# Decode attention with a gated FFN on one core: w_down as 13 rows in each partition and its last 128 rows in 32 partitions; wo's second half in 128-column matmuls

## The chip, the cores and the metric

The kernel runs on one core of one Trainium2 chip. The metric is the device time of one execution in microseconds (us); lower is better. A core has a matrix engine (TensorE, PE), a vector engine (VectorE, DVE), a scalar engine (ScalarE, ACT), GpSimd (POOL), and SyncE (SP), which here issues every DMA. Sixteen DMA engines move data between the device memory (HBM) and the 128 partitions of SBUF; matmul results go to PSUM.

## What is computed

Four tokens (B = 4), width D = 512. A gate g mixes attention over a long cache with a GEGLU FFN:

```python
g = sigmoid((x * gate_w).sum(-1, keepdims=True))
q = (x @ wq).reshape(4, 1, 32, 128).transpose(0, 2, 1, 3)
p = softmax(einsum("bhqd,bhkd->bhqk", q, k_cache) * 128 ** -0.5)   # k_cache, v_cache: 4 x 32 x 4096 x 128
a = einsum("bhqk,bhkd->bhqd", p, v_cache).transpose(0, 2, 1, 3).reshape(4, 1, 4096) @ wo   # wo: 4096 x 512
b = (gelu(x @ w_gate) * (x @ w_up)) @ w_down                       # w_gate, w_up: 512 x 1792; w_down: 1792 x 512
return g * a + (1 - g) * b
```

Everything is float32. The two caches are 268 MB each and are read once; all weights together are about 28 MB.

## The kernel before

**Attention.** There are NT = 32 steps, one for each batch row and group of four heads. A step loads a K tile and a V tile of 8 MB (128 partitions of 64 KB: 32 partitions to a head, 128 rows of 128 to a partition). DVE multiplies K by the spread query (`products`, L213) and sums over the head dimension (`sums`, L219), in two parts: 32 rows that share their place with the next K tile first (`shared`), then 96. `max_a` and `soft_max` (L224 to L242) find the maximum through PE and let ACT make the exponentials. `pv` (L267) lets PE multiply them with V into PSUM. The query comes from wq at the start (L164, `q_spread`).

**One buffer.** Weights, K and V tiles lie at hand-placed columns of one SBUF tile, `big`. K(i) is at 0 or 12288, V at VA = 28672, each 16384 columns wide. w_gate and w_up stand in V's place until V(0) is loaded. At the end wo's first half is at W0 and w_down at D0 in V's place, wo's second half at W1 = 16384, and from ES = 24576 on come the spread attention outputs (`spread`, L318) and the copy of `wide` (`fold`); both of the last lie where K(31) was.

**Queues.** The order is written by hand; the framework adds semaphore waits where data or places depend on each other. SP issues the DMAs in program order: wq, x, K(0), gate_w, w_gate, w_up, K(1), then V and K in turn, and at the end `load_w(0)` (wo's first half, 4 MB), `load_d` (w_down, 3.5 MB) and `load_w(1)` (wo's second half). The last is cut into pieces of 8, 5, 2 and 1 of its 16 rows per partition (`WO_END`), each a DMA of its own.

**FFN.** In step 0, `ffn_up` (L330) multiplies x with w_gate and then w_up: the 1792 columns are cut into four blocks of FG = 448, one in each 32-partition column group of PSUM. ACT copies the result to `fu`; `ffn_gelu` (L338) makes the product on DVE; 14 DVE transposes (L349) turn it into `hT`, so that hidden unit 14 p + i lies in partition p of slice i. After that V(0) may be loaded over w_gate and w_up.

**The end.** PE's order after the last `pv` is: 16 matmuls of wo's first half, `turn(1)`, 14 of w_down (`ffn_down`, L351), 8 of wo's second half, all by `project_wide` (L251): 512 columns at once, the n-th into column group n % 4 of the PSUM tile `wide`, so that four groups hold partial sums. Then comes `project` (L257), which cuts the 512 columns into four of 128, one for each column group of `acc`: row 8 of wo's second half, `fold` (ACT copies `wide`, and a matmul with `stack` adds its four partial sums into `acc`), rows 9 to 15. DVE copies `acc`, SP stores it. A float32 matmul appears as two records and two weight loads in the trace.

Of the kernel before, what the change touches and what calls it, by code (L numbers as in the profile page):

```python
# [9 lines left out]
F32 = mybir.dt.float32  # L10
# [7 lines left out]
def tile_gated_mix(ctx: ExitStack, tc: tile.TileContext, x, kc, vc, wq, wo, w_gate, w_up, w_down, gate_w, out):  # L18
    nc = tc.nc
    P = 128  # L20
    B, H, S, D = kc.shape
    DM = x.shape[2]
    F = w_gate.shape[1]
    KC = DM // P
# [8 lines left out]
    RJ = 4  # L33
    BP = 2
    FG = F // 4
    FC = F // P
    HW = 16
    E = HW * D // P
    GW = HW // HT
    WO_END = (0, 8, 13, 15, E)  # L40
    scale = 1.0 / math.sqrt(D)
    c_gelu = math.sqrt(2.0 / math.pi)

# [6 lines left out]
    xT = head.tile([P, KC, 4, B, 8], F32)  # L50
    kv = ctx.enter_context(tc.tile_pool(name="kv", bufs=1))
    consts = ctx.enter_context(tc.tile_pool(name="consts", bufs=1))
# [9 lines left out]
    big = kv.tile([P, VA + TW], F32)  # L62
    Q0, F0, F1, W0, D0 = VA, VA, VA + KC * F, VA, VA + TW // 2
    W1, ES = TW, TW + TW // 2

    def place(a, n):
        return big[:, a:a + n]
# [16 lines left out]
    def load_f(s):  # L84
        nc.sync.dma_start(place((F0, F1)[s], KC * F), (w_gate, w_up)[s].rearrange("(p c) n -> p (c n)", c=KC))

    def load_d():
        nc.sync.dma_start(place(D0, FC * DM), w_down.rearrange("(p i) n -> p (i n)", i=FC))

    def load_w(w):  # L90
        t = place((W0, W1)[w], E * DM)
        src = wo[w * HW * D:(w + 1) * HW * D].rearrange("(p e) n -> p (e n)", e=E)
        ends = WO_END if w else (0, E)
        for e0, e1 in zip(ends, ends[1:]):
# [34 lines left out]
    xT = xT.rearrange("p c j b k -> p c (j b k)")  # L129
# [29 lines left out]
    for c in range(KC):  # L159
        w = place(Q0 + c * H * D, H * D)  # L160
# [11 lines left out]
    stack = consts.tile([P, 32], F32)  # L172
# [71 lines left out]

    acc = ps1.tile([P, C4], F32, name="acc")
    wide = ps1.tile([P, DM], F32, name="wide")
    NW = FC + E + WO_END[1]
    nw = iter(range(NW))


    def project_wide(t, w):  # L251
        n = next(nw)
        c = n % 4
        nc.tensor.matmul(wide[32 * c:32 * c + 32, :], t, w, start=n < 4, stop=n >= NW - 4)


    def project(t, w, start, stop):  # L257
        for c in range(4):
            nc.tensor.matmul(acc[32 * c:32 * c + 32, :], t, w[:, c * C4:(c + 1) * C4], start=start, stop=stop)  # L259


    def fold():
        t = place(ES + 2 * E * 32, DM)
        nc.scalar.activation(t, wide, AF.Copy)
        project(stack, t, False, False)

    def pv(i):  # L267
        b = i % BP
# [54 lines left out]
    def attended(w, e):  # L323
        return OTS[w][:, e * 32:e * 32 + 32], place((W0, W1)[w] + e * DM, DM)


    hT = consts.tile([P, FC, 32], F32)
    fu = place(VA + 2 * KC * F, 2 * DM).rearrange("p (s n) -> p s n", s=2)

    def ffn_up(s):  # L330
        ps = ps1.tile([P, FG], F32, name="q")
        for c in range(KC):
            for j in range(4):
                nc.tensor.matmul(ps[32 * j:32 * j + 32, :], xT[:, c, :32],  # L334
                                 place((F0, F1)[s] + c * F + j * FG, FG), start=c == 0, stop=c == KC - 1)
        nc.scalar.activation(fu[:, s, :FG], ps, AF.Copy)

    def ffn_gelu():  # L338
        x1 = fu[:, 0, :FG]
        t1, t2, t3, th, y, v = (place(F1 + a * DM, FG) for a in range(6))  # L340
        nc.vector.tensor_tensor(t1, x1, x1, op=OP.mult)
        nc.vector.tensor_scalar(t2, t1, 0.044715, 1.0, op0=OP.mult, op1=OP.add)
        nc.vector.tensor_tensor(t3, t2, x1, op=OP.mult)  # L343
        nc.scalar.activation(th, t3, AF.Tanh, scale=c_gelu)
        nc.vector.scalar_tensor_tensor(y, th, 1.0, x1, op0=OP.add, op1=OP.mult)  # L345
        nc.vector.scalar_tensor_tensor(v, y, half, fu[:, 1, :FG], op0=OP.mult, op1=OP.mult)  # L346

        for i in range(FC):
            nc.vector.transpose(hT[:, i, :], v[:, i::FC])  # L349

    def ffn_down():  # L351
        for f in range(FC):
            project_wide(hT[:, f, :], place(D0 + f * DM, DM))


    load_f(0)
# [2 lines left out]
    for i in range(NT):  # L359
# [12 lines left out]
        if i == 0:  # L372
            half, gmask = gates()
            ffn_up(0)
            ffn_up(1)
            ffn_gelu()
            load_v(0)
# [14 lines left out]
        if b == 1 and g + 1 < NG:  # L392
            q_spread(g + 1)
    load_w(0)
    load_d()
    load_w(1)
    spread(0)
# [8 lines left out]
    turned(1)  # L406
    spread(1)
    ffn_down()
    for e in range(WO_END[1]):
        project_wide(*attended(1, e))  # L410
    project(*attended(1, WO_END[1]), True, False)
    fold()
    for e in range(WO_END[1] + 1, E):
        project(*attended(1, e), False, e == E - 1)
    res = work.tile([P, C4], F32, name="res", bufs=1)
    nc.vector.tensor_copy(res, acc)  # L416
# [23 lines left out]
```

## Time and profile before

The median of three runs is 1313.91 us (1313.85 to 1314.07). The profiled execution took 1313.79 us; its span, from the first to the last instruction, is 1312.0 us.

| what | value | how to read it |
|---|---|---|
| run, span | 1313.79, 1312.0 us | 1.79 us lie outside the span |
| bytes moved | 565.07 MB in 10,711 packets | a packet is one contiguous run, 64 KB for K and V |
| mean rate | 431 GB/s | over the span |
| K and V loads | 32 + 32, 29.6 and 29.2 us from issue to landing | issued about 20 us apart, so that one waits behind the other |
| wo, first half | issued 1266.72, 23.2 us to landing | |
| w_down | issued 1270.12, 28.4 us to landing | |
| wo, second half | four DMAs from 1276.44 on; 27.0, 29.6 and 30.5 us for those of 2048, 1280 and 256 KB | the fourth is issued at 1277.8 |
| DVE | 1143.2 us | L213 and L219 are 555.8 and 555.4 of it |
| granted PE clock | 0.632 in the mean | 0.5 or 1.0 at any one time |

### The profile page before, as it was taken

The numbers are of one execution on the slowest core, as the hardware profiler recorded it, in microseconds if no ns is written. First come the engines' busy times: TensorE is split into PE (matmuls) and PEld (weight loads), VectorE is DVE, ScalarE is ACT, GpSimd is POOL, SyncE is SP. The second block draws the span as 40 slices with busy tenths as digits, with TensorE's granted clock in tenths as the row PEclk, the third lists the DMA queues.
The fourth block names the chain that finished last, engine by engine and source line by source line (L and its number), as shares of the span: only waits on it lengthen the run. The fifth ranks groups of instructions, "written<-read, shape, count | busy, mean of one in ns | idle before, by whom it ended". The sixth has DMA issues, their size and how long they took to land.

```text
span 1312.0 us, 6267 instructions
## 1 busy us (share of the span) xinstructions
PE 394.9 (30%) x2680; PEld 130.9 (10%) x2680; DVE 1143.2 (87%) x261; ACT 92.6 (7%) x321; POOL 0.7 (0%) x6
## 2 busy tenths in 40 slices
PE   2403323212333321333322232322123322122337
PEld 0101001000010000110001000100001000010012
DVE  1899889988899988988989988998889898898890
ACT  0000000000000100000000000000000000000010
POOL 0000000000000000000000000000000000000000
PEclk9656666556666555666655666665566666566668
DMA  9999999999999999999999999999999999999997
GB/s 416 428 436 442 422 440 424 440 442 428 438 428 434 438 426 444 434 430 432 434 438 432 438 428 436 428 438 434 434 442 422 444 426 436 440 428 440 426 429 338
DMA packets 10711, 565.07 MB, mean 431 GB/s; under 512 B 1320, under 2 KB 1336, under 8 KB 1596
## 3 DMA queue, kind: packets, MB, share of 16 engines
q1 hardware_dynamic: 10684, 564.68, 99.5%
q8 instruction: 21, 0.34, 0.1%
q14 instruction: 6, 0.05, 0.0%
HBM read 564.67 MB, written 0.01 MB: 430 GB/s over the span
## 4 chain that ended last, share of the span: by engine, by line
DMA 72%; DVE 26%; PE 1%; issue 0%; ACT 0%; SPq 0%; DVEq 0%
DMA big<-in_A_k_cache 66%; DVE sc L219 13%; DVE big L213 12%; DMA big<-in_A_wo 2%; DMA big<-in_B_w_up 2%; DMA big<-in_A_x 2%; PE po L164 1%; PE q L334 0%; PE acc L259 0%; DVE m L233 0%; DVE hT L349 0%; DVE m L226 0%; DVE big L346 0%; DVE big L345 0%; DVE big L343 0%
## 5 line engine op out<-in xcount | busy, mean ns | idle before, releaser
L213 DVE TENSOR_TENSOR big<-big,qb 128x4096 f32<-128x4096 f32 x64 | 555.8, 8684 | 103.1 <-DMA big<-in_A_k_cache 103.1
L219 DVE TENSOR_REDUCE sc<-big 128x32 f32<-128x4096 f32 x64 | 555.4, 8678 | 1.1
L272 PE MATMUL po<-big,PM 128*32 128x512 f32 x2048 | 295.9, 742 | 437.9 <-DMA big<-in_A_v_cache 435.4
L272 PEld LDWEIGHTS po<-big,PM 128*32 128x32 f32 x2048 | 80.8, 133 | 626.7 <-issue 624.2
L235 PE MATMUL sm<-m,ones 1*128 1x4 f32 x64 | 18.7, 360 | 218.4 <-DVE m L233 218.4
L228 PE MATMUL sm<-ident,m 128*1 128x128 f32 x32 | 11.9, 371 | 214.4 <-DVE m L226 180.3
L240 ACT ACTIVATE PM<-sc,nb 32x128 f32<-32x128 f32 x128 | 67.4, 526 | 2.6
L237 ACT ACTIVATE nb<-sm 128x4 f32<-128x4 f32 x32 | 5.5, 173 | 570.3 <-PE sm L235 570.3
L235 PEld LDWEIGHTS sm<-m,ones 1*128 1x128 f32 x64 | 15.9, 306 | 238.1 <-DVE m L233 238.1
L281 ACT ACTIVATE o<-po 128x512 f32<-128x512 f32 x16 | 9.6, 597 | 326.2 <-PE po L272 326.2
L240 ACT ACTIVATION_READ_ACCUMULATOR PM<-sc,nb 32x1 f32 x128 | 26.2, 205 | 0.0
L228 PEld LDWEIGHTS sm<-ident,m 128*1 128x1 f32 x32 | 2.5, 79 | 236.9 <-issue 183.2
L200 ACT ACTIVATE qb<-q 128x512 f32<-128x512 f32 x8 | 4.8, 597 | 247.3 <-PE q L196 247.3
L128 DVE COPY xT<-sm 128x128 f32<-128x128 f32 x4 | 0.9, 283 | 20.5 <-PE sm L125 20.5
L196 PE MATMUL q<-QM,hmask 128*32 128x512 f32 x64 | 15.5, 1062 | 3.5 <-DVE QM L186 3.5
L289 PE MATMUL sm<-o,sel 128*16 128x128 f32 x128 | 15.6, 273 | 0.0
L299 DVE RECIPROCAL ri<-sm 16x1 f32<-16x1 f32 x8 | 1.2, 147 | 14.4 <-PE sm L291 14.4
L289 PEld LDWEIGHTS sm<-o,sel 128*16 128x16 f32 x128 | 11.7, 97 | 7.4 <-issue 5.0
L334 PE MATMUL q<-big,xT 128*32 128x448 f32 x64 | 9.3, 742 | 10.1 <-DMA big<-in_B_w_up 5.2
L416 DVE COPY res<-acc 128x128 f32<-128x128 f32 x1 | 0.3, 292 | 11.4 <-PE acc L259 11.4
L226 DVE TENSOR_REDUCE m<-sc 128x1 f32<-128x128 f32 x32 | 9.1, 286 | 1.1
L164 PE MATMUL po<-big,xT 128*32 128x512 f32 x64 | 9.8, 782 | 0.4 <-DVE xT L128 0.4
(61 smaller groups left out, 78.2 us busy)
## 6 DMA issues: line engine op xcount, KB each, us to landing
big<-in_A_wo SPq DMA_DIRECT2D x1, 4096.0 KB, 23.2
big<-in_B_w_gate SPq DMA_DIRECT2D x1, 3584.0 KB, 20.2
big<-in_B_w_up SPq DMA_DIRECT2D x1, 3584.0 KB, 26.5
big<-in_B_w_down SPq DMA_DIRECT2D x1, 3584.0 KB, 28.4
big<-in_A_wo SPq DMA_DIRECT2D x1, 2048.0 KB, 27.0
big<-in_A_wo SPq DMA_DIRECT2D x1, 1280.0 KB, 29.6
big<-in_A_k_cache SPq DMA_DIRECT2D x32, 29.6
big<-in_A_v_cache SPq DMA_DIRECT2D x32, 29.2
```

Source lines behind the costliest of these rows:

```text
L164: nc.tensor.matmul(PO[s][32 * j:32 * j + 32].rearrange("p j d -> p (j d)"), xT[:, c, :32], w[:, n0:n0 + HB * D], start=c == 0, stop=c == K ...
L196: nc.tensor.matmul(ps[h * PH:(h + 1) * PH].rearrange("p b d -> p (b d)"), hmask[:, j, a:a + 1].to_broadcast([P, PH]), QM.rearrange("p b d ...
L213: nc.vector.tensor_tensor(t, t, QB[g][:, b:b + 1, :].to_broadcast([P, r1 - r0, D]), op=OP.mult)
L219: nc.vector.tensor_reduce(SC[i][:, r0:r1], K(i).rearrange("p (r d) -> p r d", d=D)[:, r0:r1], axis=AX.X, op=OP.add)
L226: nc.vector.tensor_reduce(m1, SC[i], axis=AX.X, op=OP.max)
L228: nc.tensor.transpose(MT[i], m1, ident)
L235: nc.tensor.matmul(nbp, ones[:1, :], m2, start=True, stop=True)
L240: nc.scalar.activation(PM[:, PZ:].rearrange("p (c m) -> p c m", m=32)[s, :, h:RJ * HT:HT], SC[i][s, :].rearrange("p (c j) -> p c j", j=RJ) ...
L272: nc.tensor.matmul(PO[i // BP % 2][32 * c:32 * c + 32].rearrange("p j d -> p (j d)"), PM[:, m0:m0 + 32], V(i)[:, j * N:(j + 1) * N], start ...
L281: nc.scalar.activation(O[i // BP], PO[i // BP % 2], AF.Copy)
L289: nc.tensor.matmul(OS[g][:, :D], sel[:, j, m0:m0 + B * HT], O[N * g + n][:, j, :], start=(n, j) == (0, 0), stop=(n, j) == (N - 1, RJ - 1))
L334: nc.tensor.matmul(ps[32 * j:32 * j + 32, :], xT[:, c, :32], place((F0, F1)[s] + c * F + j * FG, FG), start=c == 0, stop=c == KC - 1)
```

## The change

Three things. `FC` becomes 13: w_down's rows 0 to 1663 lie 13 to a partition, and its last 128 rows lie four to a partition in the first 32 partitions (`XP`, `XC`, at column `DX` = 26624, where K(31) was), by a DMA of its own whose source is written as four by eight. `ffn_up` computes the columns in two passes: four blocks of 416, then the last 128 columns in four strided sets of 32 (column 1664 + j and every fourth after it for column group j); `hT` has 13 slices and `hX` four of 32 partitions, and `ffn_down` adds four matmuls with 32 rows each. wo's second half is no longer added to `wide`: `fold` comes first and opens `acc`, and all its 16 rows go through `project`. The pieces of its load are 9, 4, 2 and 1 rows.

```diff
-    FC = F // P
+    FC = F // P - 1
+    XP, XC = 32, P // 32
-    WO_END = (0, 8, 13, 15, E)
+    WO_END = (0, 9, 13, 15, E)
...
+    DX = ES + 4 * DM
...
     def load_d():
-        nc.sync.dma_start(place(D0, FC * DM), w_down.rearrange("(p i) n -> p (i n)", i=FC))
+        nc.sync.dma_start(place(D0, FC * DM), w_down[:P * FC].rearrange("(p i) n -> p (i n)", i=FC))
+        nc.sync.dma_start(place(DX, XC * DM)[:XP],
+                          w_down[P * FC:].rearrange("(a p i) n -> a p (i n)", a=XP // 8, i=XC))
...
-    NW = FC + E + WO_END[1]
+    NW = FC + XC + E
...
-        project(stack, t, False, False)
+        project(stack, t, True, False)
...
+    hX = consts.tile([XP, XC, 32], F32)
+    FM = 32 * FC
...
     def ffn_up(s):
         ps = ps1.tile([P, FG], F32, name="q")
-        for c in range(KC):
-            for j in range(4):
-                nc.tensor.matmul(ps[32 * j:32 * j + 32, :], xT[:, c, :32],
-                                 place((F0, F1)[s] + c * F + j * FG, FG), start=c == 0, stop=c == KC - 1)
+        w = place((F0, F1)[s], KC * F).rearrange("p (c n) -> p c n", c=KC)
+        for main in (True, False):
+            for c in range(KC):
+                for j in range(4):
+                    nc.tensor.matmul(ps[32 * j:32 * j + 32, slice(0, FM) if main else slice(FM, FG)], xT[:, c, :32],
+                                     w[:, c, j * FM:(j + 1) * FM] if main else w[:, c, P * FC + j::XC],
+                                     start=c == 0, stop=c == KC - 1)
...
-            nc.vector.transpose(hT[:, i, :], v[:, i::FC])
+            nc.vector.transpose(hT[:, i, :], v[:, i:FM:FC])
+        for j in range(XC):
+            nc.vector.transpose(hX[:, j, :], v[32 * j:32 * j + 32, FM:])
 
     def ffn_down():
         for f in range(FC):
             project_wide(hT[:, f, :], place(D0 + f * DM, DM))
+        for f in range(XC):
+            project_wide(hX[:, f, :], place(DX + f * DM, DM)[:XP])
...
     ffn_down()
-    for e in range(WO_END[1]):
-        project_wide(*attended(1, e))
-    project(*attended(1, WO_END[1]), True, False)
     fold()
-    for e in range(WO_END[1] + 1, E):
+    for e in range(E):
         project(*attended(1, e), False, e == E - 1)
```

## The prediction

> **What bounds the kernel now.** I read the page first, then the chain of waits over the last 110 us, then the end instruction by instruction, then the end in windows of 1 us.
>
> ```profile
> span 1312.0 us, 6267 instructions
> PE 394.9 (30%) x2680; PEld 130.9 (10%) x2680; DVE 1143.2 (87%) x261; ACT 92.6 (7%) x321; POOL 0.7 (0%) x6
> DMA  9999999999999999999999999999999999999997
> q1 hardware_dynamic: 10684, 564.68, 99.5%
> q8 instruction: 21, 0.34, 0.1%
> ```
> The sixteen DMA engines are busy 99.5% of the span and no compute engine is near that: bytes set the time, and the change keeps the bytes. Only the last slice is below 9, so only the end can give or lose time.
>
> ```profile
> 1276.82 29.63 DMA big<-in_A_wo
> 1306.44 0.04 issue
> 1306.49 2.30 PE acc L259 x72
> 1308.79 0.02 issue
> 1308.81 0.29 DVE res L416
> ```
> The chain ends with a transfer of wo, 72 matmul records into acc, the copy and the store. The last wo piece (256 KB) is issued at 1277.8 and takes 30.5 us: it lands at 1308.3, so the last group of acc also waits for bytes. From that landing to the end of the span are 1312.0 - 1308.27 = 3.73 us.
>
> ```profile
> 1303.00:1304.00 1.00, 1.00 (x13) 0.32 (x11) 0.00 (x0) 0.00 (x0) 0.00 (x0) 1.00 0.78 324
> 1305.00:1306.00 1.00, 0.64 (x7) 0.00 (x0) 0.00 (x0) 0.31 (x1) 0.00 (x0) 1.00 0.48 195
> 1307.00:1308.00 1.00, 1.00 (x48) 1.00 (x40) 0.00 (x0) 0.00 (x0) 0.00 (x0) 1.00 0.25 90
> ```
> The column before the last is the DMA share: it falls from 0.78 to 0.25, that is four of sixteen engines. They do not end together. Each engine adds its own completion to a DMA's semaphore, and the trace has the times. For the last piece they are, after the first at 1303.53: 0, 0.15, 0.21, 0.21, 0.43, 0.63, 1.81, 2.11, 3.03, 3.07, 3.07, 3.23, 4.46, 4.60, 4.61, 4.74. At wq they were within 0.47. Followed from load to load, an engine falls back 1.42 us whenever the instruction queue (q8) puts a 16 KB packet on it. There are 21, one for every 256 PE instructions, going round eight engines in a fixed turn; four of the eight had a third one by 1290.3 (4.5 to 4.7 behind), four had two (3.0 to 3.2 behind).
>
> **The change, part by part.**
>
> *Bytes per engine.* w_down's first part is 3,328 KB instead of 3,584: 16 KB less for each engine. A 64 KB packet takes 2.418 us, so that is 0.605 us earlier for what follows. The other 256 KB have a source of four by eight rows. The nearest row is x, whose source has four rows:
>
> ```profile
> DMA packets 40, 1.06 MB, mean 2114 GB/s; under 512 B 20, under 2 KB 20, under 8 KB 24
> ```
> From 21.8 to 22.3 us there are 20 semaphore writes (16 of wq, 4 of x) and four packets of 2 KB: x went over four engines. I take the same for the new load: 64 KB on each of four, 2.42 us; the lower bound is 0.605 (spread over sixteen), the upper 8 x 0.31 = 2.48 (the 8 KB instruction packets took 0.31). So twelve engines end 0.605 us earlier and four end 2.42 - 0.605 = 1.81 later. [...]
>
> *Which four.* I took the engines of x's four packets and followed them: they end 0.15, 2.11, 3.03 and 3.07 behind the first. Two of these identities rest on a few ns and may be wrong. The first end of the last piece moves to 1303.53 - 0.605 = 1302.93. Without the load, the latest ends at 1302.93 + 4.74 = 1307.67; the four end at 1302.93 + 2.42 + 0.15, 2.11, 3.03, 3.07 = 1305.5, 1307.5, 1308.4, 1308.4. The landing moves from 1308.27 to 1308.4: +0.1.
>
> *Instruction packets.* Thirty-two more ffn_up matmuls, 32 more for acc and 5 fewer for wide, each two records with two weight loads, are 128 + 128 - 20 = 236 more PE instructions: 5,427 records in the trace become 5,663. The 21st packet came at record 5,355, 21 short of 256 x 21. A 22nd then comes near 5,611 (bounds 5,555 and 5,634, from the other twenty), 52 before the end: about 0.7 us at 72 records per us, or 1307.1 to 1308.2. Its turn is the sixth of the eight engines, which I take to be the one of the four that ends at 1308.4. It then loses 0.92 (the time in which the fetch ran alone in earlier cases) to 1.42 (all that was lost then); bounds 0 and 1.42, I take 0.9 since only packets of 2 KB are left: the landing is 1309.3, +1.0 on before.
>
> *SP's queue.* The new load writes where K(31) lies (columns DX), so it waits for the last sums as wo's second half does:
>
> ```profile
> 1270.12 0.33 SPq L88 DMA_DIRECT2D big<-in_B_w_down  x1
> 1276.44 1.75 SPq L95 DMA_DIRECT2D big<-in_A_wo  x4
> ```
> Behind it on SP are wo's four pieces, each 0.44 us later for one more issue. Nothing: wo's first half keeps the engines busy until 1285. Uncovered it would cost the 0.44.
>
> *PE at the end.* The rows before:
>
> ```profile
> 1298.60 5.33 PE L254 MATMUL wide<-big,hT 128*32 128x512 f32 x28 [2.10 <-DMA big<-in_B_w_down]
> 1303.55 2.09 PE L254 MATMUL wide<-big 128*32 128x512 f32 x16
> 1305.69 0.60 ACT L264 ACTIVATE big<-wide 128x512 f32<-128x512 f32 x1 [7.61 <-PE wide L254]
> 1306.49 0.43 PE L259 MATMUL acc<-big 128*32 128x128 f32 x8 [0.85 <-DMA big<-in_A_wo]
> ```
> ffn_down starts 0.605 earlier, 1298.0. Four wide matmuls, one in each column group, are a round: weight-load groups 0.43 apart, two per round, give 0.86 at full clock and 1.71 at half. Thirteen matmuls of 128 rows and four of 32 put five into one column group: five rounds, 4.3 us, instead of 3.5 followed by two of wo. No row has a 32-row weight: bounds are no cost (the 13th shares its round) and a round alone for all four; five rounds hold the middle. The granted clock was 0.5 from 1299.2 to 1302.6, 3.41 us at half speed: 1.7 more. So 1304.0, copy until 1304.7. Then fold and sixteen groups of wo: 17 x 8 records x 28.5 ns (72 starts from 1306.49 to 1308.5) = 3.9, and 0.3 for the last: 1308.9 against 1308.79 before. Landing and PE meet; with the 22nd packet the landing decides. The eight wide matmuls and the fold that leave their old place were behind transfers and give nothing.
> [...]
>
> *Early.* ffn_up's second call runs 60.37 to 65.16. Narrowed to 416 of 448 columns it saves 0.3, and 32 records of 32 columns add 0.9 (28.5 ns each) to 2.3 (72 ns, the 16-column transposes at the end); the stride of four columns has no row, bounds nothing and four times 0.3. Three more 32-column DVE transposes add 3 x 0.12 (1.71 us for 14). V(0) is then issued 0.4 to 1 us after 70.3, while K(1) occupies the engines until 77.8: nothing. DVE makes it up from its 103 us of waits for K. Uncovered this would be 1 us.
>
> *Sum.* Span 1312.0 + 1.0 = 1313.0; outside the span lie 1313.79 - 1312.0 = 1.8, and the median is 0.1 above the profiled run: **1314.9**. Its own range is 1314.1 to 1315.5 (packet lost time 0 to 1.42).
>
> **Rivals.**
> 1. *The packet misses the four engines or comes after their end.* For it: its place is known to some 50 records (0.7 us), the identity to a few ns. Against: 1308.4 is the very end. Landing +0.1, PE +0.1: **1314.1**.
> 2. *The load does not do what its shape says and spreads over sixteen.* For it: both sides are contiguous and could be joined to 32 rows. Against: x. Landing as before, PE at 1308.9: **1314.0**.
> 3. *The four engines are all early ones.* Against: the following above. The last landing is 1307.67; PE must then not pass half clock: 1308.2 at its end, **1313.3**.
> 4. *Slower: PE's late work runs at half clock.* Place: fold and the sixteen groups of wo now all stand behind wide's copy. PE idles 0.75 us there and again for wo's first piece, after 1.5 us before ffn_down. If a window with both halves the clock from 1304, seventeen groups take 0.43 instead of 0.23 each: 3.4 more, **1317.3**; from 1306, half of it. It decides once wo's groups, not the landing, end last: 1 us of half clock. For it: the 2.1 us that sufficed. Against: full clock from 1302.6 to the end before.
>
> **How the numbers follow.** Forecast 0.45, first rival 0.25, second 0.12, third 0.08, fourth 0.10. The range from 1313.2 to 1316.4 leaves out most of the fourth and some mishap below. Over 0.2% is 2.6 us, about what a measurement of this kernel can tell from no change: faster than 1311.3 none of the cases gives (0.02 for what I don't see); slower than 1316.5 the fourth in most of its course, 0.09; the rest, 0.89, within.
>
> **What would show it.** Four packets' worth of 8 KB rows on four engines, DMA share near 0.25 or below until 1308 to 1309, twelve engines ending by 1307.7; w_down's first landing near 1298.0; 136 records for acc in some 4 us; a 22nd packet of q8 in the last 2 us; PE clock 1.0 after 1303. I am wrong if all engines end by 1307.7, if the landing is past 1310, or if PE ends over 1 us after the last landing.

## The result and the profile after

| | before | changed |
|---|---|---|
| median | 1313.89 us (1313.65 to 1314.31, 15 runs) | 1316.45 us (1315.65 to 1317.68, 15 runs) |
| profiled execution, its span | 1313.79, 1312.0 us | 1315.93, 1314.2 us |
| last landing of wo (its last completion) | 1308.27 | 1310.49 |

The forecast was 1314.9 us (1313.2 to 1316.4). The ratio is 1.0020, 95% interval [1.0012, 1.0027]: the change makes the kernel 2.6 us slower, 2.2 of them in the profiled execution, and its last landing is 2.2 us later as well. So one question is left: what holds up the transfers?

The page of the changed kernel, beside the page lines of before in the prediction:

```profile
span 1314.2 us, 6508 instructions
PE 394.4 (30%) x2798; PEld 132.6 (10%) x2798; DVE 1143.9 (87%) x264; ACT 92.6 (7%) x321; POOL 0.7 (0%) x6
...
DMA packets 10760, 565.09 MB, mean 430 GB/s; under 512 B 1336, under 2 KB 1352, under 8 KB 1612
...
q1 hardware_dynamic: 10732, 564.68, 99.5%
q8 instruction: 22, 0.36, 0.1%
```
The bytes are those of before but for 0.02 MB of instructions, and the engines are still busy 99.5% of a longer span. PE has 118 more records of each kind, 236 in all, as forecast. Packets went from 10,711 to 10,760: 32 rows of 8 KB, one instruction packet and 16 semaphore writes. Sixteen writes mean that the new load ran on sixteen engines and not on four.

The chain of waits at the end, with start, length and what it was:

```profile
1277.87 31.99 DMA big<-in_A_wo
1309.86 0.04 issue
1309.90 1.10 PE acc L264 x24
1311.00 0.02 issue
1311.03 0.29 DVE res L428
```
The same kind of chain as before, but the last transfer in it is now wo's third piece, which lands at 1309.86 (1307.65 before), and no longer the second (1306.44 before), and three groups are left behind it instead of nine. The transfers set the end more than before.

The same stretches in windows, first before, then changed. The columns are busy time of PE, PEld, DVE, ACT and POOL, granted PE clock, DMA share, GB/s:

```profile
1293.00:1297.00 4.00, 3.50 (x40) 1.61 (x32) 0.42 (x2) 0.00 (x0) 0.00 (x0) 1.00 0.95 407
1297.00:1301.00 4.00, 2.40 (x16) 0.72 (x20) 0.42 (x1) 0.63 (x1) 0.00 (x0) 0.78 0.98 420
```

```profile
1293.00:1297.00 4.00, 3.24 (x37) 1.48 (x28) 0.69 (x2) 0.00 (x0) 0.00 (x0) 1.00 1.04 340
1297.00:1301.00 4.00, 1.65 (x8) 0.40 (x12) 0.16 (x1) 0.63 (x1) 0.00 (x0) 0.70 0.98 278
1301.00:1303.00 2.00, 2.00 (x20) 0.59 (x13) 0.00 (x0) 0.00 (x0) 0.00 (x0) 0.75 0.97 416
```
This is the line that matters. The DMA share stays at 0.98, but the engines move 278 GB/s instead of 420, and from 1301 on 416 again. The shortfall is 67 GB/s x 4 us + 142 GB/s x 4 us = 836 KB, which at 430 GB/s is 1.9 us, most of the 2.2. Engines that were busy thus did not move bytes at their usual rate: their packets took longer. Packet by packet, in the stretch from 1293 to 1301 us:

| packet | usual | longest in the changed kernel |
|---|---|---|
| 26,624 B (w_down's 13 rows) | 0.99 us | 1.55 us |
| 18,432 B (wo's first piece) | 0.69 us | 1.70 us |
| 8,192 B (the new load) | 0.31 us | 0.80 us |

Summed over all packets there, the excess over the usual times is 36 engine-us (microseconds of one of the sixteen engines), 36 / 16 = 2.2 us for each. All sixteen engines end late: put in order, the completions of the last piece move by 2.1 to 2.5 us, and one of them by 3.3. The first moves from 1303.53 to 1305.94, the last from 1308.27 to 1310.49.

PE's part of the end, in the timeline (start, length, instruction, idle time before and what ended it):

```profile
1299.35 4.91 PE L259 MATMUL wide<-big,hT 128*32 128x512 f32 x26 [3.10 <-DMA big<-in_B_w_down]
...
1304.19 1.06 PE L259 MATMUL wide<-big,hX 32*32 32x512 f32 x8
1305.32 0.60 ACT L269 ACTIVATE big<-wide 128x512 f32<-128x512 f32 x1 [7.50 <-PE wide L259]
1305.97 0.43 PE L264 MATMUL acc<-big,stack 128*32 128x128 f32 x8 [0.72 <-ACT big L269]
...
1308.68 2.28 PE L264 MATMUL acc<-big 128*32 128x128 f32 x56 [0.25 <-DMA big<-in_A_wo]
```
w_down's main part releases PE at 1299.35, 0.75 later than before, though it has 16 KB less per engine. The 26 + 8 records take 5.9 us, and wo's groups then wait for pieces of wo.

### The profile page after: what moved, and what is told of

It reads as the page before. It is cut to its first block, busy times and chain, and to the rows that moved or that the text cites. A ratio compares the mean times of both kernels' runs of the same rounds, so it can differ in the third digit from the quotient of the medians.

```text
span 1314.2 us, 6508 instructions
## 1 busy us (share of the span) xinstructions
PE 394.4 (30%) x2798; PEld 132.6 (10%) x2798; DVE 1143.9 (87%) x264; ACT 92.6 (7%) x321; POOL 0.7 (0%) x6
## 2 busy tenths in 40 slices
DMA packets 10760, 565.09 MB, mean 430 GB/s; under 512 B 1336, under 2 KB 1352, under 8 KB 1612
## 3 DMA queue, kind: packets, MB, share of 16 engines
q1 hardware_dynamic: 10732, 564.68, 99.5%
## 4 chain that ended last, share of the span: by engine, by line
DMA 71%; DVE 28%; issue 0%; SPq 0%; PE 0%; ACT 0%; DVEq 0%
DMA big<-in_A_k_cache 69%; DVE big L218 14%; DVE sc L224 14%; DMA big<-in_A_wo 2%; DVE m L238 0%; DVE hT L360 0%; PE acc L264 0%; DVE m L231 0%; SPq L100 0%; DVE big L357 0%; DVE hX L362 0%; DVE big L354 0%; DVE big L356 0%; DVE big L352 0%; ACT big L355 0%
## 5 line engine op out<-in xcount | busy, mean ns | idle before, releaser
L344 PE MATMUL q<-big,xT 128*32 128x32 f32 (+1 forms) x128 | 11.0, 516 | 8.2 <-DMA big<-in_B_w_gate 4.8
```

Source lines behind the costliest of these rows:

```text
L344: nc.tensor.matmul(ps[32 * j:32 * j + 32, slice(0, FM) if main else slice(FM, FG)], xT[:, c, :32], w[:, c, j * FM:(j + 1) * FM] if main el ...
```

## The experiments

The theory that I formed after the result: the 256 KB written to partitions 0 to 31 hold up every packet in flight beside them, because of where they are written. The rivals: the new load's packets of 8 KB are slow whatever they are written to; its engines (sixteen or four) are the cause; PE's new order, or the wo part, is; or the bytes themselves. All edits are against the changed kernel except in e4. "Before" had medians of 1313.95 (e1 to e4), 1313.82 (e5 to e8) and 1313.76 (e9, e10) beside them.

| run | median (range, runs), us | ratio to before [95%] | last landing | packets |
|---|---|---|---|---|
| e1_rows128 | 1314.17 (1313.84 to 1315.45, 11) | 1.0003 [0.9994, 1.0012] | 1308.32 | usual |
| e2_every4th | 1331.66 (1330.55 to 1331.78, 4) | 1.0133 [1.0119, 1.0146] | 1308.03 | usual |
| e3_four_engines | 1315.59 (1315.27 to 1316.80, 11) | 1.0013 [1.0004, 1.0021] | 1310.64 | stretched |
| e4_wo128_only | 1313.83 (1313.66 to 1314.70, 11) | 1.0000 [0.9991, 1.0009] | 1308.60 | usual |
| e5_no_load | 1313.67 (1313.08 to 1314.48, 11) | 0.9997 [0.9988, 1.0005] | 1307.74 | usual |
| e6_64parts | 1316.66 (1315.93 to 1317.78, 11) | 1.0020 [1.0011, 1.0029] | 1310.45 | stretched |
| e7_parts96 | 1316.66 (1315.80 to 1317.29, 11) | 1.0020 [1.0011, 1.0029] | 1310.77 | stretched |
| e8_split_only | 1316.45 (1316.01 to 1318.17, 11) | 1.0021 [1.0012, 1.0030] | 1310.49 | stretched |
| e9_load_twice | 1318.06 (1317.61 to 1318.74, 5) | 1.0033 [1.0020, 1.0045] | 1312.68 | stretched more |
| e10_row_each | 1313.62 (1313.43 to 1314.11, 11) | 0.9999 [0.9990, 1.0008] | 1308.19 | usual |

### e1: the same bytes, one row to each of 128 partitions

```diff
-        nc.sync.dma_start(place(DX, XC * DM)[:XP],
-                          w_down[P * FC:].rearrange("(a p i) n -> a p (i n)", a=XP // 8, i=XC))
+        nc.sync.dma_start(place(DX, DM), w_down[P * FC:])
```


> The changed kernel, but w_down's last 128 rows are loaded one to each of 128 partitions (128 packets of 2 KB) instead of four to each of 32; the four matmuls still read the first 32 partitions at 2048 columns, so that their operand is other data. Destination theory (the 2.4 us come from sixteen engines writing into 32 partitions): the packets of w_down and wo beside it take their usual 0.99 and 0.69 us, the last landing comes back to about 1308.3, and the run is 1314.0 to 1314.6, what is left being PE's end. Source theory (a contiguous stretch of 256 KB read by all engines at once): as the changed kernel, 1316.0 to 1317. PE theory (wo in 128-column matmuls behind the copy): about 1316, with the landing early and PE late.

The windows of this run:

```profile
1293.00:1297.00 4.00, 3.34 (x40) 1.52 (x32) 0.59 (x2) 0.00 (x0) 0.00 (x0) 1.00 1.00 424
1297.00:1301.00 4.00, 2.81 (x20) 0.86 (x24) 0.25 (x1) 0.63 (x1) 0.00 (x0) 0.75 1.00 421
```
424 and 421 GB/s: every packet of w_down's 13 rows and of wo has its usual time (0.99 and 0.69 us for the two large sizes), and of the new load's 128 packets all but four take the usual 0.08. The loss is gone with the rest of the change in place. Now PE sets the end, as its chain shows:

```profile
1304.56 0.61 ACT big L268
1305.17 0.04 issue
1305.21 3.96 PE acc L263 x136
1309.17 0.02 issue
1309.20 0.29 DVE res L427
```
The fold and sixteen groups run 3.96 us without a wait. But this edit changes two things, the destination and the packet (2 KB instead of 8 KB); e2 was to separate them.

### e2: 8 KB packets to every fourth partition

```diff
-        nc.sync.dma_start(place(DX, XC * DM)[:XP],
-                          w_down[P * FC:].rearrange("(a p i) n -> a p (i n)", a=XP // 8, i=XC))
+        nc.sync.dma_start(place(DX, XC * DM)[::4], w_down[P * FC:].rearrange("(p i) n -> p (i n)", i=XC))
```


> The changed kernel, but the last 128 rows go four to each of 32 partitions that are four apart (0, 4, ... 124): the same 32 packets of 8 KB and the same source, another destination; the four matmuls still read partitions 0 to 31, so that their operand is other data. Destination theory: no stretched packets, 1314.0 to 1314.6. Source theory, or a price of 8 KB packets: 1316.0 to 1317 as the changed kernel.

The time misses every expectation, by 15 to 17 us, and for another reason, in the timeline:

```profile
1298.39 0.63 ACT L324 ACTIVATE big<-t 128x512 f32<-128x512 f32 x1 [49.24 <-DMA big<-in_B_w_down]
```
ACT's `spread`, which puts the attention output in front of the new load's columns, stood idle for 49 us until that load had landed, and everything on the path to the output waited with it. The columns do not overlap (`spread` ends at column 25600, DX begins at 26624); I take it that the framework kept track of the strided partitions as a larger region, which I did not test. The time says nothing of the load, but its transfers ran as planned:

```profile
1293.00:1297.00 4.00, 0.00 (x0) 0.00 (x0) 0.00 (x0) 0.00 (x0) 0.00 (x0) 0.50 0.99 422
1297.00:1301.00 4.00, 0.00 (x0) 0.00 (x0) 0.00 (x0) 2.53 (x9) 0.00 (x0) 0.50 1.00 425
```
The packets are the changed kernel's in number and size (10,760, of them the same 32 of 8 KB), at 422 and 425 GB/s, none stretched. So 8 KB packets alone are not it, nor is the source, which both read in the same order. PE idles in these windows; e1 had PE busy, but with packets of 2 KB. Between them they leave open a cause that needs 8 KB packets and a busy PE together; e7 settles it.

### e3: four engines in fact

```diff
-                          w_down[P * FC:].rearrange("(a p i) n -> a p (i n)", a=XP // 8, i=XC))
+                          w_down[P * FC:].rearrange("(p a i) n -> a p (i n)", a=XP // 8, i=XC))
...
-                    nc.tensor.matmul(ps[32 * j:32 * j + 32, slice(0, FM) if main else slice(FM, FG)], xT[:, c, :32],
-                                     w[:, c, j * FM:(j + 1) * FM] if main else w[:, c, P * FC + j::XC],
+                    rest = w[:, c, P * FC:].rearrange("q (p a i) -> q i a p", a=XP // 8, i=XC)
+                    to = ps[32 * j:32 * j + 32, FM:].rearrange("q (a p) -> q a p", a=XP // 8)
+                    nc.tensor.matmul(ps[32 * j:32 * j + 32, :FM] if main else to, xT[:, c, :32],
+                                     w[:, c, j * FM:(j + 1) * FM] if main else rest[:, j],
```


> The changed kernel, but the source rows are taken in another order (partition 8a + p holds group 4p + a, and ffn_up's columns likewise), so that four by eight can't be joined: I expect four engines with eight packets of 8 KB each. As the prediction had it: four engines 1.81 us later, twelve 0.605 earlier, landing 1308.4 to 1309.3, 1314.1 to 1315.5. [...] If the load still spreads over sixteen: 1316.5.

The changed kernel's source, written as four by eight rows, is contiguous and was run as 32 rows on sixteen engines. Here the rows of a block lie apart, so that nothing can be joined, and the load does run on four engines: 12 of its completions come at once and four later, and the trace has 12 fewer semaphore writes (1,324 packets under 512 B instead of 1,336). This is the kernel that the prediction costed. It took 1315.59 us, 0.7 above the forecast for it, and it too has stretched packets (26,624 B up to 1.87 us) and a last landing at 1310.64, where the forecast for four engines was 1308.4. The windows:

```profile
1293.00:1297.00 4.00, 3.88 (x44) 1.75 (x36) 0.37 (x2) 0.00 (x0) 0.00 (x0) 1.00 1.04 316
1297.00:1301.00 4.00, 1.01 (x8) 0.35 (x12) 0.76 (x2) 0.63 (x1) 0.00 (x0) 0.83 0.94 323
```
316 and 323 GB/s: the number of engines does not decide whether the others are held up.

### e4: the wo part alone

```diff
-    WO_END = (0, 8, 13, 15, E)
+    WO_END = (0, 9, 13, 15, E)
...
-    NW = FC + E + WO_END[1]
+    NW = FC + E
...
-        project(stack, t, False, False)
+        project(stack, t, True, False)
...
-    for e in range(WO_END[1]):
-        project_wide(*attended(1, e))
-    project(*attended(1, WO_END[1]), True, False)
     fold()
-    for e in range(WO_END[1] + 1, E):
+    for e in range(E):
```


> The kernel before with wo's part of the change alone (fold first, all sixteen rows of wo's second half in 128-column matmuls, pieces of 9, 4, 2 and 1 rows); w_down as before. Destination theory: no stretched packets, the last landing stays at 1308.3 and PE ends within 0.5 us of before: 1313.7 to 1314.6. PE theory: most of the change's 2.6 us, 1315.5 to 1316.5.

1313.83 us, ratio 1.0000 [0.9991, 1.0009]. The 128-column matmuls for wo cost nothing that can be told from no change; the interval is about 1 us to either side.

### e5: the new load left out

```diff
-        nc.sync.dma_start(place(DX, XC * DM)[:XP],
-                          w_down[P * FC:].rearrange("(a p i) n -> a p (i n)", a=XP // 8, i=XC))
```


> The changed kernel without the load of w_down's last 128 rows (256 KB less to move); the four matmuls read what K left there. Shows what the change would be worth if that load cost nothing. The twelve-engines sum of the prediction: last landing 1307.7, PE's end (about 1309.2 in the span of the kernel with one row to a partition) then sets the time: 1313.6 to 1314.2. If landing alone set the end: 1313.3.

1313.67 us, and the last landing is 1307.74. With 256 KB less this is a base line for the load's price: 1310.49 - 1307.74 = 2.75 us for the load as the change has it, about what its bytes over sixteen engines (0.605) and the stretching counted above (2.2) add up to. In e1 and e10 the same bytes cost 0.58 and 0.45. These are differences of single profiled runs, good to some 0.3 us: before and e4 move the same bytes and land at 1308.27 and 1308.60.

### e6, e7: other parts of the partitions

```diff
-        nc.sync.dma_start(place(DX, XC * DM)[:XP],
-                          w_down[P * FC:].rearrange("(a p i) n -> a p (i n)", a=XP // 8, i=XC))
+        nc.sync.dma_start(place(DX, 2 * DM)[:64], w_down[P * FC:].rearrange("(p i) n -> p (i n)", i=2))
```


> The changed kernel, with the last 128 rows two to each of partitions 0 to 63 (64 packets of 4 KB over sixteen engines); the four matmuls read partly other data. If the price goes with the number of partitions written, it is half or less: 1314.8 to 1315.6. [...] No price: 1314.2.

```diff
-        nc.sync.dma_start(place(DX, XC * DM)[:XP],
-                          w_down[P * FC:].rearrange("(a p i) n -> a p (i n)", a=XP // 8, i=XC))
+        nc.sync.dma_start(place(DX, XC * DM)[96:], w_down[P * FC:].rearrange("(p i) n -> p (i n)", i=XC))
```


> The changed kernel, with the last 128 rows four to each of partitions 96 to 127 instead of 0 to 31; the four matmuls read what K left in 0 to 31. If any 32 adjacent partitions are the cause: 1315.8 to 1317, with stretched packets. [...]

Both took 1316.66 us, within 0.3 of the changed kernel's time, with stretched packets. The chain that ended last goes in both from the landing of w_down's main part (1299.44 and 1300.17, in e1 1298.14) through PE, not through wo's last pieces; both are late. e6 in windows:

```profile
1293.00:1297.00 4.00, 2.59 (x32) 1.34 (x24) 0.84 (x2) 0.46 (x1) 0.00 (x0) 1.00 1.05 337
1297.00:1301.00 4.00, 1.51 (x8) 0.40 (x12) 0.00 (x0) 0.17 (x1) 0.00 (x0) 0.55 0.94 261
```
337 and 261 GB/s with twice the partitions and packets of 4 KB: twice as many neighbouring partitions do not help, and 8 KB is not needed. That partitions 96 to 127 cost the same shows that nothing is special about the first 32, and that what else is read or written in 0 to 31 is not the cause.

e7 also settles what e2 left open. From 1297.30 to 1300.20 us no compute engine works in it. The same stretch in e7, then in e2:

```profile
1297.30:1300.20 2.90, 0.00 (x0) 0.00 (x0) 0.00 (x0) 0.00 (x0) 0.00 (x0) 0.50 0.91 234
```

```profile
1297.30:1300.20 2.90, 0.00 (x0) 0.00 (x0) 0.00 (x0) 1.75 (x6) 0.00 (x0) 0.50 1.05 448
```
PE idles in both, and the rate is 234 GB/s in e7 and 448 in e2. Of the packets that lie wholly in the stretch, in e7 all 17 of wo and all 10 of the new load take longer than usual, in e2 none of 48 and 22. The two kernels load the same 32 packets of 8 KB from the same source to the same columns and differ in nothing but the partitions (and in 1.75 us of ACT's work, in e2, where nothing is stretched), so the partitions are the cause, and a busy PE is not needed.

So loads of the same 256 KB to partitions 0 to 31, 0 to 63 and 96 to 127 stretch the packets beside them (the changed kernel, e6 and e7, last landings of 1310.45 to 1310.77), and loads to every fourth of 128 (e2, 1308.03) or to all 128 (e1 and e10, 1308.32 and 1308.19) do not.

### e8: the w_down part alone

```diff
-    WO_END = (0, 9, 13, 15, E)
+    WO_END = (0, 8, 13, 15, E)
...
-    NW = FC + XC + E
+    NW = FC + XC + E + WO_END[1]
...
-        project(stack, t, True, False)
+        project(stack, t, False, False)
...
+    for e in range(WO_END[1]):
+        project_wide(*attended(1, e))
+    project(*attended(1, WO_END[1]), True, False)
     fold()
-    for e in range(E):
+    for e in range(WO_END[1] + 1, E):
```


> The change of w_down and ffn_up alone; wo's second half as before (8 rows by 512-column matmuls, pieces of 8, 5, 2 and 1). Destination theory: the whole loss is here, 1315.8 to 1317. If wo's part shares in it (PE's end behind the late landing): 1314.8 to 1315.6.

1316.45 us, the changed kernel's time: the loss is in w_down's part. This kernel has 21 instruction packets like the one before, so the 22nd has no share in it.

### e9: the load twice

```diff
+        nc.sync.dma_start(place(DX, XC * DM)[64:64 + XP],
+                          w_down[P * FC:].rearrange("(a p i) n -> a p (i n)", a=XP // 8, i=XC))
```


> The changed kernel with the suspected cost doubled: the same 256 KB are loaded a second time, into partitions 64 to 95 at the same columns (nothing reads them). If each such load costs by itself what the first did (0.6 us of bytes and about 2.2 of stretched packets): 1318.5 to 1320. If the second, which goes to the other half of the partitions, evens out what the first left uneven: 1316.5 to 1317.5. Bytes alone: 1317.0.

1318.06 us, 1.6 more than the changed kernel, between the expectations. The last landing is 1312.68, 4.94 after e5's. Its bytes are twice 0.605 = 1.21; the summed excess of its packets is 61 engine-us, 61 / 16 = 3.8; together 5.0. The account of e5 (bytes plus stretched packets) holds here too. The second load added 25 engine-us to the first one's 36.

### e10: the change with a row to each partition

```diff
-        nc.sync.dma_start(place(DX, XC * DM)[:XP],
-                          w_down[P * FC:].rearrange("(a p i) n -> a p (i n)", a=XP // 8, i=XC))
+        nc.sync.dma_start(place(D0 + FC * DM, DM), w_down[P * FC:])
...
-    NW = FC + XC + E
+    NW = FC + 1 + E
...
-                                     w[:, c, j * FM:(j + 1) * FM] if main else w[:, c, P * FC + j::XC],
+                                     w[:, c, j * FM:(j + 1) * FM] if main else w[:, c, P * FC + 32 * j:P * FC + 32 * j + 32],
...
-        for j in range(XC):
-            nc.vector.transpose(hX[:, j, :], v[32 * j:32 * j + 32, FM:])
+        nc.vector.transpose(hT[:, FC, :], v[:, FM:])
...
-        for f in range(FC):
+        for f in range(FC + 1):
             project_wide(hT[:, f, :], place(D0 + f * DM, DM))
-        for f in range(XC):
-            project_wide(hX[:, f, :], place(DX + f * DM, DM)[:XP])
```


> The changed kernel mended: the last 128 rows one to each of 128 partitions, next to the thirteen (place D0, before wo's second half in the queue and with no wait for K), a fourteenth slice of hT in place of hX, fourteen matmuls of 128 rows; wo's part of the change kept. Destination theory: unstretched packets and a last landing at 1308.3, PE's end earlier than with the four 32-row matmuls: 1313.7 to 1314.3, no difference from before.

1313.62 us, ratio 0.9999 [0.9990, 1.0008]. The load goes to other columns here, behind the thirteen rows, and is issued at 1269.89, since it need not wait for K (1276.56 in the changed kernel); e1 kept the place and the wait. Its windows:

```profile
1293.00:1297.00 4.00, 2.92 (x36) 1.40 (x28) 0.84 (x2) 0.13 (x1) 0.00 (x0) 1.00 0.99 416
1297.00:1301.00 4.00, 2.96 (x16) 0.80 (x20) 0.00 (x0) 0.49 (x1) 0.00 (x0) 0.62 1.00 423
```
Both parts of the change, the split included, cost nothing that can be told once the split-off rows go to all 128 partitions. Nothing is won against the kernel before either: its bytes are the same.

## Why the prediction was wrong, point by point

**The step that failed** is the price of the new load: "I take the same for the new load: 64 KB on each of four, 2.42 us; the lower bound is 0.605 (spread over sixteen), the upper 8 x 0.31 = 2.48". It failed in two ways. The assumption about engines was wrong: sixteen completions show a spread over sixteen, which the second rival had (a source that "could be joined to 32 rows"). x, the row that it was taken from, has four rows in all and could not show whether four by eight are joined. That alone is not the failure, since e3, with four engines in fact, lands at 1310.64 and not at 1308.4. The larger part is that both bounds price the load by bytes and packets on its own engines; where in SBUF it is written, and what it does to the packets of w_down and wo around it, was not asked. Measured against e5 the load costs 2.75 us on all sixteen engines, above the upper bound, which was meant for four engines only. The load over all partitions costs 0.45 to 0.58 (e10, e1), about the lower bound.

**The sign was luck.** The forecast's 1.0 us over before was 0.1 for four late engines and 0.9 for a fetched instruction packet. Neither was paid, and what made the kernel slower stands in none of its terms.

**Which four, and the 22nd instruction packet.** There were no four. The packet was there (22 in the row of q8), but at 1310.2, later than the 1307.1 to 1308.2 forecast since PE was late too. All packets of the last piece took their usual 0.08 us beside it, so I take it that its engine had finished; the spread of that piece's completions is 4.55 us instead of 4.74. The 0.9 us booked for it was not paid, and e8 without it is as slow.

**Bytes per engine.** Right: without the load the latest completion was forecast at 1307.67, and e5 has 1307.74.

**SP's queue.** Right in size and in being hidden: wo's first piece is issued at 1276.93 instead of 1276.44, while the engines were busy with wo's first half.

**PE at the end.** Five rounds with half clock were forecast as 4.3 + 1.7 = 6.0 us; the changed kernel has 5.9. The granted clock was half again, from 1298.57 to 1301.98; it fell within the 3.10 us for which PE stood idle. In the kernel before, PE idled 2.10 us there, from 1296.5 to 1298.6, and the clock was half from 1299.22 to 1302.64. In e1, which idled 1.85 us there, it fell as well and the 26 records took 5.32 us; in e5, which idled 1.09, it stayed at 1.00 and they took 3.62. The start of ffn_down was forecast for 1298.0: e1 and e5 have 1298.19 and 1297.93, the changed kernel has 1299.35. The fold and sixteen groups were forecast as 3.9 and 0.3; e1 has 3.96 in all. "Landing and PE meet" holds: in the changed kernel the pieces of wo decide, in e1 PE.

**Early work.** ffn_up's second call takes 4.82 us instead of 4.79, so the narrow passes cost about the 0.3 that the narrower blocks save, and not 0.9 to 2.3; the transposes take 2.39 us instead of 1.71, twice the 0.36 more that I had booked; V(0) is issued at 71.07 instead of 70.30, within the 0.4 to 1 us forecast and, as forecast, without effect.

**Rivals.** The second had the spreading right and its time wrong (1314.0), for the same reason as the forecast; e1 and e10, where the load is spread and nothing is stretched, took 1314.17 and 1313.62. The fourth, on the slow side, had the sign and not the cause: PE's late work ran at full clock from 1302 on. The text named a landing past 1310 as what would show it wrong; it was 1310.49.

**What stays open** is the size and the mechanism. By their bytes over sixteen engines the 256 KB take 0.605 us; 2.2 more were measured. Packets that go to other partitions at the same time wait as well: wo's first piece has 128 packets of 18,432 bytes, one to each partition, of which 32 go to partitions 0 to 31, and 67 of the 128 took over 0.02 us longer than the usual 0.69, up to 1.70. By what mechanism they wait is not shown; the runs show which sets of partitions stretch packets and which do not.

## What to carry to other kernels

A load's price is not only its bytes: where transfers set the time, a load to part of the partitions (32 or 64 neighbours) can slow what is in flight beside it (here to 278 instead of 420 GB/s; the load cost 2.7 to 3.0 us, and 0.45 to 0.58 when written to all partitions), so write such a remainder as one short row to each of the 128 partitions, or look at GB/s and packet times beside the DMA share. A share of 0.98 with the rate down by a third was the sign of it here. And read from the semaphore's completions how many engines a DMA ran on (here sixteen, where four were booked) before building on the shape in which its source is written.

## What the runs showed of the hardware beyond that

- A 256 KB load to 32 or 64 neighbouring partitions moved the last landing by 2.7 to 3.0 us against none (changed kernel, e6, e7), the same load to 128 partitions by 0.45 to 0.58 (e10, e1).
- A source of four by eight contiguous rows ran on sixteen engines (16 semaphore writes), the same bytes in an order that can't be joined on four (12 completions at once, then four).
- With PE idle for 3.10 us ahead of ffn_down, for 2.10 (the kernel before) or for 1.85 (e1), its clock fell to half for 3.4 us; with 1.09 us (e5) it did not fall.
